# Causal mask, batch order and second-chunk gates at the start of an mLSTM and GELU kernel

## The chip, the cores and the metric

The kernel runs on one core of a Trainium2 chip. A core has five engines that each take their own instructions in order: TensorE (PE; the loading of its weights is shown apart as PEld), VectorE (DVE), ScalarE (ACT), GpSimd (POOL) and SyncE (SP). All DMAs of this kernel are issued by SP. The engines wait for each other by semaphores. The metric is the device time of one execution in microseconds (us), as the median of several runs. The profile is that of one execution.

## The reference

Two stages follow each other. The first is an mLSTM cell over 4 batches, 8 heads, 768 steps and a head width of 40:

```python
for t in range(S):
    m_new = np.maximum(f_gate[:, :, t] + m, i_gate[:, :, t])
    f_stab = np.exp(f_gate[:, :, t] + m - m_new)
    i_stab = np.exp(i_gate[:, :, t] - m_new)
    m = m_new
    C = f_stab[:, :, None, None] * C + i_stab[:, :, None, None] * np.einsum('bhd,bhe->bhde', vt, kt)
    n = f_stab[:, :, None] * n + i_stab[:, :, None] * kt
    h_tilde = np.einsum('bhde,bhe->bhd', C, qt)
    nq = np.einsum('bhd,bhd->bh', n, qt)[:, :, None]
    denom = np.maximum(np.abs(nq), 1.0)
    o = 1.0 / (1.0 + np.exp(-o_gate[:, :, t]))
    y[:, :, t] = o * h_tilde / denom
```

Its result is laid out as 3072 tokens of 320 values and goes through a feed-forward block of width 2048:

```python
h = x @ w_in
g = h * (1.0 / (1.0 + np.exp(-1.702 * h)))
return (g @ w_out).astype(np.float32)
```

q, k, v and the gates come in 32-bit floats, the two weight matrices in 64-bit floats.

## The kernel before

**Chunks.** The 768 steps are cut into 6 chunks of 128 (`w`), and each chunk is done for all 4 batches. Inside a chunk the recurrence is replaced by matrices: decay weights between each pair of steps, times the scores of k and q, times v, plus what the state of the earlier chunks gives. Between chunks `new_states` and `carry` bring the state on.

**The attention steps of a batch.** `transposes(w, b)` makes kT and qT (in chunk 0 by TensorE into p_t and a copy by ScalarE, line 316). `weights(0, b)` builds the exponents of the decay weights in PSUM by matmuls with `pick`, m3 and a3 (lines 333 and 334), and ScalarE takes their exp (line 335); then GpSimd's `affine_select` (line 342) sets to zero what lies in the future. `scores` multiplies k by q into p_s (line 353), and VectorE multiplies the result into the weights (line 355). `values` multiplies by v into p_o (line 365), and VectorE makes y of it with the denominator and the output gate (lines 388 to 394); GpSimd copies 64 columns of y to fill its last third (line 396). `seam` transposes y into p_x (line 403), and ScalarE copies it to xT (line 404). `columns` makes the per-step factors, and `scale_values` multiplies v by some of them on GpSimd (line 410), for the states.

**The gates.** `gates(w)` (lines 245 to 287) runs scans on VectorE. For chunk 0 it also splits two rows into three bf16 parts each: a3 with GpSimd, m3 with VectorE. For later chunks it sends the row m_run to DRAM (m_row), and `spread` loads it back to all partitions.

**The weights.** The 64-bit numbers are turned into 32-bit ones on the chip. `fetch(n)` loads piece n (512 KB), and `convert(n)` makes it on ScalarE (two instructions, "A", lines 233 and 234) and then on VectorE (four, "V", lines 237 to 242). Pieces 0 to 9 belong to w_in, 10 to 19 to w_out. Hidden blocks j = 0 and 1 need the pieces 0, 1 and 2, blocks 2 and 3 the pieces 2, 3 and 4.

**The feed-forward steps.** `up(w, j, n)` multiplies xT by w_in for n pairs of hidden blocks: `full` for the first 256 of the 320 rows (line 467), `rest` for the last 64 (line 473), then the GELU on ScalarE (line 477). `down` multiplies by w_out. The attention of the next chunk is woven into `down`.

**What sets the order.** The order is written by hand: every engine, and SP's queue of DMAs, takes its instructions in the order in which the program names them, and a pool's buffers come round in that order too. p_t, p_w, p_s, p_o, p_x, p_cols and p_c share one pool of four PSUM buffers, ps_a. Chunk 0 is written out, from `gates(0)` to `gate_out(3)`: the steps of the four batches interleaved with `convert(0)`, `convert(1)` and `convert(2)` and with `keep_busy`, matmuls of zeros that keep TensorE running. Then `up(0, 0, 2, between)` does hidden blocks 0 and 1 in two halves: for the first two batches (columns 0 to 255) as soon as their xT is there, with `values(0, 2)`, `values(0, 3)`, both `seam`s and two conversions called in between (the three functions of `between`), and then for the last two. `gates(1)` comes after it, and then SP's loads of k for the next chunk.

At the start SP loads, in this order: gates of chunk 0; k and q of batch 0 and of batch 1; piece 0; v and o of batch 0; k and q of batch 2; v and o of batch 1; piece 1; k and q of batch 3; piece 2; v and o of batches 2 and 3; pieces 3, 4 and 5; gates of chunk 1; pieces 6 to 9.

GpSimd clears, in this order: padding of k_st and q_bl, a column of v_st set to one, then after the gates of chunk 0 state and k_bl, and q_bl once more after the first `up`. VectorE makes `pick` (line 201) and then `half`, `dec_in`, `par` and `pair` (lines 207 to 213), which the gates and columns of later chunks need, ahead of `gates(0)`.

Of the kernel before, what the change touches and what calls it, by code (L numbers as in the profile page):

```python
# [8 lines left out]
FP = mybir.dt.float32  # L9
U32 = mybir.dt.uint32  # L10
BF = mybir.dt.bfloat16
# [11 lines left out]
L = 128  # L23
# [11 lines left out]
def kernel(  # L35
# [131 lines left out]


    load_gates(0)
    for what, n in (("kq", 0), ("kq", 1), (fetch, 0), ("vo", 0), ("kq", 2), ("vo", 1), (fetch, 1), ("kq", 3), (fetch, 2),  # L170
                    ("vo", 2), ("vo", 3), (fetch, 3), (fetch, 4), (fetch, 5)):
        if what is fetch:
            fetch(n)
        else:
            load(0, what, slice(n, n + 1))
    load_gates(1)
    for n in range(6, 10):
        fetch(n)

# [18 lines left out]
    for j in range(3):  # L200
        V.tensor_scalar(out=pick[j * BH:(j + 1) * BH, :], in0=ident[0:BH, 0:BH], scalar1=-1.0, scalar2=None,
                        op0=OP.mult)


    half = const.tile([3 * BH, 2, 64], FP, name="half")
    dec_in = const.tile([3 * BH, 2, BH // 2], FP, name="dec_in")
    V.memset(half, 0.0)
    V.memset(dec_in, 0.0)
    par = const.tile([BH, 2], FP, name="par")
    pair = const.tile([BH, BH // 2], FP, name="pair")  # L210
    V.tensor_reduce(out=par, in_=ident[0:BH, 0:BH].rearrange("p (j two) -> p two j", two=2), axis=AX.X, op=OP.add)
    V.tensor_reduce(out=pair, in_=ident[0:BH, 0:BH].rearrange("p (j two) -> p j two", two=2), axis=AX.X, op=OP.add)
    V.tensor_copy(out=half[0:BH], in_=par.unsqueeze(2).to_broadcast([BH, 2, 64]))
    for t in (k_st, q_st):
        G.memset(t[:, :, D:DP], 0.0)

    a3 = const.tile([3 * BH, L], BF, name="a3")
    m3 = const.tile([3 * BH, L], BF, name="m3")
# [106 lines left out]
    def weights(w, b):  # L325
        if w == 0:
            x = wt[w, b] = work.tile([L, NP, 2, L], FP, tag="wt", bufs=4, name="wt")
            for i in range(2):
                pw = ps_a.tile([L, NP, L], FP, tag="a", name="p_w")
                for p in range(NP):  # L330
                    h = b * H + 2 * p + i
                    one = pick[:, h:h + 1].to_broadcast([3 * BH, L])
                    T.matmul(pw[:, p, :], one, m3, start=True, stop=False)
                    T.matmul(pw[:, p, :], a3, one, start=False, stop=True)
                A.activation(out=x[:, :, i, :], in_=pw, func=AF.Exp)
        else:
            x = wt[w, b].rearrange("s p i t -> s (p i) t")
            for h in range(H):
                A.activation(out=x[:, h, :], in_=x[:, h, :], func=AF.Exp, scale=-1.0,  # L339
                             bias=cols[w][:, b * H + h:b * H + h + 1])  # L340
        x = wt[w, b].rearrange("s p i t -> s (p i) t")
        G.affine_select(out=x, in_=x, compare_op=OP.is_ge, fill=0.0, base=0, pattern=[[0, H], [1, L]],  # L342
                        channel_multiplier=-1)
        if w and b == 0:
            A.activation(out=eo[w], in_=eo[w], func=AF.Tanh, scale=0.5)

    def scores(w, b):
# [9 lines left out]
    def values(w, *bs, states=False):  # L357
        po, pi = {}, {}
        for b in bs:
            po[b] = ps_a.tile([L, H, D1], FP, tag="a", name="p_o")  # L360
            for p in range(NP):
                for i in range(2):
                    h = 2 * p + i
                    for t in HALVES:
                        T.matmul(po[b][t, h, :], wt[w, b][:, p, i, t], v_st[:, b * H + h, :], start=True, stop=True)  # L365
        for b in bs if w else ():
            pi[b] = ps_a.tile([L, H, D1], FP, tag="a", name="p_i")
            for p in range(NP):
                for t in HALVES:
                    T.matmul(pi[b][t, 2 * p:2 * p + 2, :].rearrange("p a b -> p (a b)"), qT[w, b][:, p, t],  # L370
                             state[:, b * NP + p].rearrange("p a b -> p (a b)"), start=True, stop=True)
        if states:

            for b in bs:
                scale_values(w, b)
            new_states(w)
            for b in bs:
                scale_state(w, b)
        for b in bs:
            u = po[b]  # L380
            if w:
                u = work.tile([L, H, D1], FP, tag="u", name="u")
                g = cols[w][:, BH + b * H:BH + (b + 1) * H].unsqueeze(2).to_broadcast([L, H, D1])
                V.tensor_tensor(out=u, in0=pi[b], in1=g, op=OP.mult)
                V.tensor_tensor(out=u, in0=po[b], in1=u, op=OP.add)

            den = work.tile([L, H, 1], FP, tag="den", name="den")
            V.tensor_scalar(out=den, in0=u[:, :, D:D1], scalar1=-1.0, scalar2=1.0, op0=OP.mult, op1=OP.max)
            V.tensor_tensor(out=den, in0=u[:, :, D:D1], in1=den, op=OP.max)
            V.reciprocal(out=den, in_=den)  # L390
            z = eo[w][:, b * H:(b + 1) * H, :]
            V.scalar_tensor_tensor(out=z, in0=z, scalar=1.0, in1=u[:, :, 0:D], op0=OP.add, op1=OP.mult)
            y = ys[w, b] = work.tile([L, DM + 64], FP, tag="y", name="y")
            V.scalar_tensor_tensor(out=y[:, 0:DM].rearrange("p (h d) -> p h d", d=D), in0=z, scalar=0.5,
                                   in1=den.to_broadcast([L, H, D]), op0=OP.mult, op1=OP.mult)
            G.tensor_copy(out=y[:, DM:DM + 64], in_=y[:, DM - 64:DM])
# [55 lines left out]
    def up(w, j, n, between=None, states=False):  # L452

        x = xT[w].rearrange("p c b t -> p c (b t)")
        begin, end = range(j, j + n // 2), range(j + n // 2, j + n)
        ph = {}
        ts = slice(0, W)

        def take(j, pool, tag):
            ph[j] = [pool.tile([128, W], FP, tag=tag, name="p_h") for _ in range(2)]

        def full(j, first):
            for c in range(2):
                for i in range(2):
                    T.matmul(ph[j][i][:, ts], w_half[i][c][:, j // 2, j % 2 * 128:(j % 2 + 1) * 128], x[:, c, ts],  # L467
                             start=(first and c == 0), stop=(not first and c == 1))

        def rest(j, first):  # L470
            for i in range(2):
                r = slice(i * 64, i * 64 + 64)
                T.matmul(ph[j][i][:, ts], w_in_x[r, j, :], x[r, 2, ts], start=first, stop=not first)

        def gelu(j):
            for i, g in enumerate(hidden_of(w, j)):
                A.activation(out=g, in_=ph[j][i], func=AF.Gelu_apprx_sigmoid)  # L477

        if between:
            take(j, ps_m, "m")  # L480
            take(j + 1, ps_x, "x")
            ts = slice(0, W // 2)
            full(j, True)
            between[0]()
            rest(j, False)
            rest(j + 1, True)
            between[1]()
            full(j + 1, False)
            between[2]()
            ts = slice(W // 2, W)  # L490
        for k in begin:
            if k not in ph:
                take(k, *((ps_m, "m") if k == j else (ps_x, "x")))
            full(k, True)
        if states:
            new_states(w)
            carry(w)
# [197 lines left out]
        z = eo[0][:, b * H:(b + 1) * H, :]  # L695
        A.activation(out=z, in_=z, func=AF.Tanh, scale=0.5)

    G.memset(v_st[:, :, D:D1], 1.0)
    gates(0)
    G.memset(state, 0.0)  # L700
    G.memset(k_bl, 0.0)
    transposes(0, 0)
    weights(0, 0)
    transposes(0, 1)
    convert(0, "A")
    scores(0, 0)
    weights(0, 1)
    keep_busy(2)
    convert(0, "V")
    scores(0, 1)  # L710
    keep_busy(2)
    gate_out(0)
    transposes(0, 2)
    values(0, 0)
    weights(0, 2)
    keep_busy(2)
    gate_out(1)
    convert(1, "A")
    values(0, 1)
    scores(0, 2)  # L720
    seam(0, 0)
    transposes(0, 3)
    weights(0, 3)
    convert(1, "V")
    seam(0, 1)
    convert(2)
    scores(0, 3)
    columns(0)
    gate_out(2)
    gate_out(3)  # L730


    beside = {0: ((5,), range(10, 16)), 1: ((6, 7, 8), ()), 2: ((9, 10, 11), (16, 17)), 3: ((12, 13, 14), (18, 19)),
# [14 lines left out]
    for w in range(NW):  # L748
        more = w + 1 < NW
        for j in range(NF // 2):  # L750
            if j % 2 == 0:
# [4 lines left out]
                        else:  # L756
                            up(w, j, 4, states=(j == 0))
                elif j == 0:
                    up(w, j, 2, (lambda: values(0, 2), lambda: values(0, 3),
                                 lambda: (seam(0, 2), seam(0, 3), convert(3), convert(4))))  # L760
                    for b in range(B):
                        scale(0, b)
                    weights_in(0)
                else:
                    weights_in(j // 2)
                    up(w, j, 2, states=(j == 2))
            if j == 0 and more:
                load(w + 1, "o")
            if w == 0 and j == 0:
                gates(1)  # L770
                load_blocks(1, 0)
                spread(1)
            if w == 1 and j == 1:
# [2 lines left out]
            if more:  # L776
# [7 lines left out]
                        spread(w + 1)  # L784
                if j == (4 if w else 6):
                    load(w + 1, "k")
                if w == 0 and j == 0:
                    G.memset(q_bl, 0.0)
                if w == 1 and 4 <= j < 6:
                    transposes(w + 1, 2 * j - 8)  # L790
                    transposes(w + 1, 2 * j - 7)
# [68 lines left out]
```

## Time and profile before

| | us |
|---|---|
| median of 5 runs | 494.01 |
| lowest and highest run | 493.92 and 496.68 |
| the profiled execution's own time | 494.01 |
| its span in the profile | 492.3 |
| TensorE busy | 482.8 |
| VectorE busy | 332.5 |
| ScalarE busy | 207.1 |
| GpSimd busy | 69.2 |

The span runs from the first to the last recorded instruction. Busy time is a mean over stages that differ, so it has to be read by stage. In a timeline a row gives the start, the duration, the engine, the source line, the operation with what it writes and reads, and how many instructions the row merges; in brackets stands how long the engine had idled before and what ended the idling. A matmul of 32-bit numbers is two records, so "x16" can be eight instructions. A row of waits gives the time in total, the number of waits and the longest.

### The profile page before, as it was taken

The numbers are of one execution on the slowest core, as the hardware profiler recorded it, in microseconds if no ns is written. First come the engines' busy times: TensorE is split into PE (matmuls) and PEld (weight loads), VectorE is DVE, ScalarE is ACT, GpSimd is POOL, SyncE is SP. The second block draws the span as 40 slices with busy tenths as digits, with TensorE's granted clock in tenths as the row PEclk, the third lists the DMA queues.
The fourth block names the chain that finished last, engine by engine and source line by source line (L and its number), as shares of the span: only waits on it lengthen the run. The fifth ranks groups of instructions, "written<-read, shape, count | busy, mean of one in ns | idle before, by whom it ended". The sixth has DMA issues, their size and how long they took to land. (4 is left out here: it accounts for less than half of the span.)

```text
span 492.3 us, 10268 instructions
## 1 busy us (share of the span) xinstructions
PE 482.8 (98%) x4030; PEld 387.5 (79%) x4030; DVE 332.5 (68%) x817; ACT 207.1 (42%) x533; POOL 69.2 (14%) x109
## 2 busy tenths in 40 slices
PE   8899999999999999999999999999999999999997
PEld 5674457775446999877999877999977999877897
DVE  6879985882792777686696586786666776244841
ACT  4557668311224700465901374910354930155400
POOL 7240001231000332000232000242000030000000
PEclk9999999999999999999999999999999999999999
DMA  9999799403699610796300497300194000000000
GB/s 148 177 253 352 87 278 164 60 15 67 73 166 206 78 34 3 120 246 74 31 28 3 88 259 84 40 23 8 49 270 43 2 1 28 28 0 3 0 28 27
DMA packets 175952, 44.85 MB, mean 91 GB/s; under 512 B 164352, under 2 KB 169504, under 8 KB 175904
## 3 DMA queue, kind: packets, MB, share of 16 engines
q1 hardware_dynamic: 175904, 44.21, 48.2%
q8 instruction: 31, 0.51, 0.4%
q14 instruction: 17, 0.14, 0.1%
HBM read 40.17 MB, written 4.01 MB: 90 GB/s over the span
## 5 line engine op out<-in xcount | busy, mean ns | idle before, releaser
L643 PE MATMUL p_out<-w_out_sb,g 128*128 128x160 f32 x480 | 69.8, 301 | 0.0
L404 ACT COPY xT<-p_x 128x384 f32<-128x384 f32 x24 | 11.0, 481 | 134.3 <-PE p_x L403 134.3
L643 PEld LDWEIGHTS p_out<-w_out_sb,g 128*128 128x128 f32 x480 | 66.3, 190 | 1.3 <-issue 0.5
L467 PE MATMUL p_h<-xT,w_in_sb 128*128 128x512 f32 (+1 forms) x144 | 58.1, 553 | 2.1 <-ACT xT L404 1.2
L342 POOL TENSOR_SCALAR_AFFINE_SELECT wt<-wt 128x1024 f32<-128x1024 f32 x24 | 27.2, 1132 | 230.2 <-ACT wt L339 226.8
L552 DVE TENSOR_TENSOR g<-p_u,g 128x256 f32<-128x256 f32 x64 | 27.2, 424 | 40.8 <-PE p_u L544 32.8
L467 PEld LDWEIGHTS p_h<-xT,w_in_sb 128*128 128x128 f32 x144 | 26.4, 190 | 31.5 <-issue 26.8
L648 DVE TENSOR_TENSOR o_sb<-o_sb,p_out 128x160 f32<-128x160 f32 x70 | 21.4, 317 | 41.2 <-PE p_out L643 40.9
L549 ACT COPY g<-p_u 128x256 f32<-128x256 f32 x96 | 34.4, 377 | 34.5 <-PE p_u L544 31.2
L339 ACT ACTIVATE wt<-wt,cols 128x128 f32<-128x128 f32 x160 | 48.0, 397 | 0.0
L556 ACT ACTIVATE g<-g 128x256 f32<-128x256 f32 x96 | 33.9, 425 | 31.3 <-DVE g L552 31.3
L355 DVE TENSOR_TENSOR wt<-p_s,wt 128x512 f32<-128x512 f32 x48 | 30.5, 683 | 11.0 <-POOL wt L342 9.1
L592 PE MATMUL p_out<-w_out_sb,g 128*128 128x320 f32 x128 | 36.2, 437 | 0.0
L643 PE MATMUL p_out<-t,big 128*128 128x160 f32 x240 | 35.5, 301 | 0.0
L477 ACT ACTIVATE g<-p_h 128x512 f32<-128x512 f32 x32 | 17.9, 598 | 38.7 <-PE p_h L467 20.0
L643 PEld LDWEIGHTS p_out<-t,big 128*128 128x128 f32 x240 | 33.3, 190 | 0.2
L592 PEld LDWEIGHTS p_out<-w_out_sb,g 128*128 128x128 f32 x128 | 23.8, 190 | 10.1 <-issue 0.5
L544 PE MATMUL p_u<-xT,w_in_sb 128*128 128x256 f32 x128 | 31.2, 382 | 0.0
L544 PE MATMUL p_u<-xs,big 128*128 128x256 f32 x128 | 30.3, 379 | 0.0
L572 PE MATMUL p_v<-xT,w_in_x 64*128 64x512 f32 x64 | 29.6, 602 | 0.0
L572 PE MATMUL p_u<-xT,w_in_x 64*128 64x512 f32 x64 | 29.6, 602 | 0.0
L365 PEld LDWEIGHTS p_o<-v_st,wt 128*64 128x64 f32 x768 | 24.1, 138 | 5.1 <-issue 2.7
(156 smaller groups left out, 852.8 us busy)
## 6 DMA issues: line engine op xcount, KB each, us to landing
wt<-m_row SPq DMA_DIRECT2D x20, 512.0 KB, 6.2
out_dram<-o_sb SPq DMA_DIRECT2D x24, 160.0 KB, 1.8
eo<-in_o_gate_dram SPq DMA_DIRECT2D x5, 640.0 KB, 5.6
v_st<-in_v_dram SPq DMA_DIRECT2D x5, 640.0 KB, 8.8
k_st<-in_k_dram SPq DMA_DIRECT2D x5, 640.0 KB, 11.1
big<-in_moe_w_in_dram SPq DMA_DIRECT2D x5, 512.0 KB, 5.9
big<-in_moe_w_out_dram SPq DMA_DIRECT2D x8, 320.0 KB, 4.5
k_bl<-in_k_dram SPq DMA_DIRECT2D x40, 64.0 KB, 2.7
```

The source lines that it names most:

```text
L339: A.activation(out=x[:, h, :], in_=x[:, h, :], func=AF.Exp, scale=-1.0, bias=cols[w][:, b * H + h:b * H + h + 1])
L342: G.affine_select(out=x, in_=x, compare_op=OP.is_ge, fill=0.0, base=0, pattern=[[0, H], [1, L]], channel_multiplier=-1)
L355: V.tensor_tensor(out=wt[w, b][:, :, i, :], in0=pw[i], in1=wt[w, b][:, :, i, :], op=OP.mult)
L365: T.matmul(po[b][t, h, :], wt[w, b][:, p, i, t], v_st[:, b * H + h, :], start=True, stop=True)
L467: T.matmul(ph[j][i][:, ts], w_half[i][c][:, j // 2, j % 2 * 128:(j % 2 + 1) * 128], x[:, c, ts], start=(first and c == 0), stop=(not first ...
L544: T.matmul(p[k][:, ts[t]], a[:, k // 2, k % 2 * 128:(k % 2 + 1) * 128], b, start=first, stop=True, skip_group_check=True)
L549: A.copy(out=g[k][i][:, ts[t]], in_=chain[k][:, ts[0]])
L552: V.tensor_tensor(out=g[k][i][:, ts[t]], in0=p[k][:, ts[pt]], in1=g[k][i][:, ts[t]], op=OP.add)
L556: A.activation(out=dst, in_=dst if src is None else src, func=AF.Gelu_apprx_sigmoid)
L572: T.matmul(p[k], w_in_x[r, k, :], x[r, 2, :], start=False, stop=True, skip_group_check=True)
L592: T.matmul(po, gs[w, f // 2][:, f % 2, b * L:(b + 1) * L], w_out_sb[:, f, :], start=(f == 0), stop=(f == NF - 1))
L643: T.matmul(po, a(f), b[:, f, :], start=(f == 0), stop=(f == NH - 1))
```

## The change

1. **Mask.** In chunk 0 the causal mask is added to the exponents by TensorE: each group of four heads in PSUM starts with one matmul of a bf16 identity (`ident_bf`) with a bf16 matrix `not_yet`, which holds −1e30 where the step lies in the future and zero elsewhere. The matmuls for the heads add to it. The select on GpSimd after the exp is gone for chunk 0 and stays for the others. VectorE clears `not_yet` and makes `ident_bf`; GpSimd's `affine_select` fills `not_yet`. Both lie in `xs`, which is free then.
2. **Order of chunk 0.** Batches 0 and 1 go all the way to xT first (weights, scores, values, seam), and then batches 2 and 3. `convert(0)` on VectorE comes behind the y of both, `convert(1)` behind it; `convert(2)` moves behind the last seam. Both scores of batches 2 and 3 come before any of hidden blocks 0 and 1.
3. **The first `up`.** `between` is now one function. `full` for columns 0 to 255 of blocks 0 and 1 comes first, then `rest_of_first` (`values` of batches 2 and 3 together, both seams, conversions 2, 3 and 4), then `full` for columns 256 to 511, then `rest` for all columns. `scale` is called per batch earlier, and `values(0, 2, 3, states=True)` scales v of batches 2 and 3.
4. **Second chunk's gates.** `load_gates(1)` moves ahead of v and o of batch 0, and `gates(1)` into chunk 0's order, between `transposes(0, 1)` and `scores(0, 0)`; with it its DMA of m_row moves ahead of the loads of pieces 10 to 15.
5. **Loads.** Order now: gates of chunk 0; k and q of batches 0 and 1; gates of chunk 1; v and o of batches 0 and 1; piece 0; k and q of batch 2; piece 1; k and q of batch 3; v and o of batches 2 and 3; pieces 2 to 9.
6. **Clearings.** k_bl's clearing and v_st's column of ones move ahead of `gates(0)`, state's behind the values of batch 0; the second clearing of q_bl is gone. `half`, `dec_in`, `par` and `pair` are made behind `gates(0)`.

```diff
@@ loads
+    for what, n in (("kq", 0), ("kq", 1), (load_gates, 1), ("vo", 0), ("vo", 1), (fetch, 0), ("kq", 2), (fetch, 1),
+                    ("kq", 3), ("vo", 2), ("vo", 3), *((fetch, n) for n in range(2, 10))):
@@ before gates(0)
     for t in (k_st, q_st):
         G.memset(t[:, :, D:DP], 0.0)
+    G.memset(v_st[:, :, D:D1], 1.0)
+    G.memset(k_bl, 0.0)
+
+    not_yet, ident_bf = (xs.bitcast(BF)[:, i * L:(i + 1) * L] for i in range(2))
+    V.memset(not_yet, 0.0)
+    G.affine_select(out=not_yet, in_=not_yet, compare_op=OP.is_ge, fill=NEG, base=0, pattern=[[1, L]],
+                    channel_multiplier=-1)
+    V.tensor_copy(out=ident_bf, in_=ident)
@@ weights(0, b)
+                T.matmul(pw, ident_bf, not_yet.unsqueeze(1).to_broadcast([L, NP, L]), start=True, stop=False)
                 for p in range(NP):
                     h = b * H + 2 * p + i
                     one = pick[:, h:h + 1].to_broadcast([3 * BH, L])
-                    T.matmul(pw[:, p, :], one, m3, start=True, stop=False)
-                    T.matmul(pw[:, p, :], a3, one, start=False, stop=True)
+                    T.matmul(pw[:, p, :], one, m3, start=False, stop=False)
+                    T.matmul(pw[:, p, :], a3, one, start=False, stop=(p == NP - 1))
                 A.activation(out=x[:, :, i, :], in_=pw, func=AF.Exp)
+            return
@@ the order of chunk 0, after
+    gates(0)
+    (half, dec_in, par, pair)
+    transposes(0, 0)
+    weights(0, 0)
+    transposes(0, 1)
+    gates(1)
+    scores(0, 0)
+    weights(0, 1)
+    scores(0, 1)
+    gate_out(0)
+    gate_out(1)
+    values(0, 0)
+    G.memset(state, 0.0)
+    convert(0, "A")
+    values(0, 1)
+    keep_busy(2)
+    seam(0, 0)
+    transposes(0, 2)
+    convert(0, "V")
+    seam(0, 1)
+    convert(1, "A")
+    weights(0, 2)
+    keep_busy(2)
+    transposes(0, 3)
+    weights(0, 3)
+    convert(1, "V")
+    columns(0)
+    gate_out(2)
+    gate_out(3)
+    scale(0, 0)
+    scale(0, 1)
+    scores(0, 2)
+    scores(0, 3)
+
+    def rest_of_first():
+        values(0, 2, 3, states=True)
+        seam(0, 2)
+        seam(0, 3)
+        for n in (2, 3, 4):
+            convert(n)
@@ up, with between
+            begin, end = (j, j + 1), ()
         for k in begin:
+            take(k, *((ps_m, "m") if k == j else (ps_x, "x")))
+            full(k, True, slice(0, W // 2 if between else W))
+        if between:
+            between()
+            for k in begin:
+                full(k, True, slice(W // 2, W))
@@ after the first up
-                gates(1)
                 load_blocks(1, 0)
                 spread(1)
...
-                if w == 0 and j == 0:
-                    G.memset(q_bl, 0.0)
```

## The prediction

> **What bounds the kernel now.** I read the page's head first, then the busy time by stage, then TensorE's waits from 44 us to the end, then the timelines of the first 45 us. Two lines of the page and the windows:
>
> ```profile
> span 492.3 us, 10268 instructions
> ...
> PE 482.8 (98%) x4030; PEld 387.5 (79%) x4030; DVE 332.5 (68%) x817; ACT 207.1 (42%) x533; POOL 69.2 (14%) x109
> ```
>
> ```profile
> core 0: us, PE busy (x) PEld busy (x) DVE busy (x) ACT busy (x) POOL busy (x), PEclk, DMA share, GB/s
> 0.00:10.00 10.00, 8.15 (x44) 4.64 (x44) 7.65 (x26) 3.76 (x6) 6.98 (x19) 1.00 0.91 146
> 10.00:20.00 10.00, 8.14 (x130) 6.50 (x130) 6.46 (x13) 5.59 (x12) 3.58 (x5) 1.00 1.21 180
> 20.00:25.80 5.80, 5.62 (x83) 4.91 (x80) 4.73 (x11) 4.61 (x10) 1.88 (x3) 1.00 1.00 160
> 25.80:40.00 14.20, 12.83 (x120) 9.92 (x120) 11.35 (x21) 8.17 (x18) 5.99 (x8) 1.00 0.99 278
> 40.00:44.20 4.20, 3.89 (x12) 1.35 (x13) 3.79 (x8) 4.20 (x9) 0.00 (x0) 1.00 1.06 397
> 44.20:116.00 71.80, 71.80 (x522) 45.91 (x523) 57.09 (x116) 33.54 (x75) 10.61 (x16) 1.00 0.63 129
> ```
>
> The waits of TensorE from 44 us to the end:
>
> ```profile
> PE p_h L467 <- ACT xT L404: 0.6, 1, 0.6
> PE p_out L643 <- DVE o_sb L648: 0.4, 1, 0.4
> ```
>
> From 44.2 us on TensorE has no gap up to 116 and 1.0 us of waits in all. So nothing that the change does to work beside TensorE after 44 us (gates of the second chunk, SP's queue, the clearing of q_bl) can gain more than that 1.0 us. The change is worth what it does to one moment: when `new_states(0)` (p_c, line 429) may start, 44.13 us now. Everything behind it follows at TensorE's pace.
>
> TensorE on the way there:
>
> ```profile
> 24.58 1.18 PE L353 MATMUL p_s<-qT,kT 40*128 40x128 f32 x16
> ...
> 32.94 0.82 PE L403 MATMUL p_x<-ident,y 128*128 128x128 f32 x6
> 34.38 1.99 PE L467 MATMUL p_h<-xT,w_in_sb 128*128 128x256 f32 x8 [0.62 <-ACT xT L404]
> ...
> 39.95 1.95 PE L467 MATMUL p_h<-xT,w_in_sb 128*128 128x512 f32 x4 [0.59 <-DVE w_in_sb L242]
> 42.21 1.98 PE L467 MATMUL p_h<-xT,w_in_sb 128*128 128x512 f32 x4 [0.31 <-DVE w_in_sb L242]
> ```
>
> The last scores end at 25.76; 18.4 us later p_c starts. The loads bound the first part, as the view of q's tile shows: q of batch 3 was issued at 14.40 and took the longest of the four, 7.9 us, so it landed at 22.3.
>
> ```profile
> DMA to landing us min/median/max: 3.9/4.6/7.9
> ```
>
> The start, on GpSimd and VectorE:
>
> ```profile
> 1.31 0.74 POOL L215 MEMSET k_st<- 128x768 f32 x1
> 1.99 0.74 POOL L215 MEMSET q_bl<- 128x768 f32 x1
> 2.67 0.16 POOL L698 MEMSET v_st<- 128x32 f32 x1
> ...
> L201 DVE TENSOR_SCALAR pick<-ident x3: 173/173/1449, 1.4 to 3.1; 32x32 bf16<-32x32 f32 x3
> ```
>
> The first of three equal `pick` copies took 1449 ns, from 1.40 to 2.85, the others 173: it ended when GpSimd's three clearings did (2.67 + 0.16 = 2.83).
>
> **What the Trainium skill says.** "SBUF — State Buffer", section Who interferes with whom: VectorE in a two-port mode and GpSimd share one port pair, held for a whole instruction while the other blocks. The 1449 ns agree, and so does the shift of line 238 at 35.66, 2.58 us against 0.43 elsewhere, while q_bl is cleared (36.17 to 37.97). "TensorE: Matmul & The Clock Gate", section What's actually happening: the clock falls after about 3.4 us of idling. No gap here is that long and every slice shows full clock; my longest gap below is 2 us.
>
> **The change, part by part.**
>
> *Mask on TensorE.* Removed: four GpSimd selects of 1.09 to 1.50 us between exp and the scores' product (line 342, first chunk). Only batch 0's lay on the path: the product waited for it from p_s's end at 11.08 to 12.20, 1.1 us. Added: eight matmuls 128x512 bf16. The trace has that shape as p_idle, two in 0.60 us; estimate 0.22 to 0.30 each, 2.1 us in all, of which per batch one stands before data that is late anyway and one, 0.22, on the path. Without that cover a batch costs 0.6.
>
> *k_bl's clearing moved ahead of gates(0), half's making behind it.* The clearing takes 1.80 us (q_bl's row, same shape) and now follows v_st's at 2.83 back to back, to about 4.6. `pick` is two-port, and all three copies must be through before not_yet's clearing, the bf16 identity and the gate scans. Pick's first copy was passed over at two such boundaries in this trace; even if it slips in at the third, the next two block. So picks end at 4.6 + 0.39 = 5.0 (3.22 before); not_yet and identity 0.4; gates(0) starts at 5.4 instead of 3.75: 1.65 late. Bounds: 0 (VectorE slips in ahead of k_bl each time) to 2.0 (the new select blocks it too). I take 1.65. The making of half (0.44 us, 3.31 to 3.75) moves behind gates(0).
>
> *Through the first two batches.* a3 is ready 4.3 after the gates start (3.75 to 8.04 before): 9.7. Weights(0,0): 9.7 to 10.9, exp to 11.5. Scores 11.6 to 12.8. VectorE meanwhile does gates(0) to 10.1, half to 10.5, gates(1) 2.4 (44.43 to 46.8 before) to 12.9: its move costs the product nothing, with 0.1 to spare; its two loads (issued at 4.3, about 4.5 to land) are there at 8.9. On SP these two, 32 KB, pass ahead of v and o, whose batch 0 then lands near 10 and is wanted at 15.7; fetch(0) lands near 14 and is wanted by ScalarE at 15.4. Products 13.0 to 14.2; scores(0,1) 13.7 to 14.9 (0.75 behind the products' start, as at 12.95); products to 16.3; p_o; the y chains of 1.47 each to 17.7 and 19.1 (21.6 + 0.5 = 22.1 before, since convert(0) stood ahead). TensorE's p_x at 17.95 and 19.45; ScalarE copies xT, kT, qT, xT to 20.55, convert(1) to 21.65, exp(0,2) to 22.7.
>
> *Batches 2 and 3.* The same loads stand ahead of q's last one, in another order, so it lands at 22.3 again. Transposes to 22.95, qT to 23.7, exp(0,3) to 24.75, columns to 25.05 (p_s's fourth buffer). The last scores end at 26.6: 0.8 late. So half of the 1.65 is won back by the mask and the order, and 22.3 + 3.4 = 25.7 is the best that this load allows.
>
> *The middle.* Now four half blocks (full(0), full(1), 3.85 us by twice the 1.92 of eight records) go ahead of p_o(2) and p_o(3): 26.6 to 30.45; p_o to 32.6 (1.13 each). Then nothing is left on TensorE to cover the y chains: y of batch 2 to 33.05, of batch 3 to 34.5 (1.47 each), the pad copy and p_x to 35.3, ScalarE's xT to 35.9; second halves from 36.0. Before, full(1), rest(0) and rest(1) lay in those holes, and the second halves started at 34.38. Then 3.85 + rest at full width 1.99 = 5.85 (before 4.98, from 34.38 to 39.36, and 0.59 of waiting): full(2) at 41.85, its second half at 43.8, p_c at **45.75**. VectorE's three conversions after xT(3): start 36.5, 2.36 each, 43.6; just in time. They no longer meet GpSimd's scale and clearing, which cost line 238 2.15 us.
>
> Sum at p_c: +0.8 (last scores 26.6 against 25.76), +0.8 (from them to the second halves 9.4 against 8.6: y chains uncovered), 0 (from there to p_c 9.75 both times: 0.87 more of rest against waits of 0.59 and 0.31 gone) = 45.75 − 44.13 = **+1.6 us**.
>
> *Second chunk.* SP waited 4.1 us for the gates at m_row and then issues k_bl; that goes, and q_bl comes some 4 us earlier. VectorE's wait for it (2.8 us, up to 79.74) shrink, but TensorE has no gap: 0. VectorE loses 2.4 us of gates between conversions 4 and 6; with PE 1.6 later, its lead grows from 1.8 us (w_in piece 6 at 49.2, wanted at 51.0). So no new stall. q_bl's clearing (1.80) and GpSimd's freed time: 0.
>
> Span 492.3 + 1.6 = 493.9; the run took 494.01 around that span, and this is also the median, so **495.6**.
>
> **The rivals.**
>
> A. The hold is carried in full. If the two-port casts of gates(0) or the handovers in the longer chain win nothing back, scores end at 27.4 or later, and +1.65 +0.8 or more gives 2.5 to 3.5: **497.0**, slower by over 0.5%. For it: about fourteen handovers follow one another. Against: mask and convert(0) leave the path. It decides from scores ending at 27.5.
>
> B. q of batch 3 lands later. p_t is ready for it at 22.2, so each microsecond is paid in full; at 23.2 or later it makes +2.5: **496.7**. For it: it took 7.9 us, and the queue is full (share 0.9 to 1.2). Against: the same bytes ahead.
>
> C. No hold, and k and q flow faster with fetch(2) behind them: scores end at 25.0 to 25.8, and only the middle's +0.8 is left, or a little less: −1 to +0.4, **494.2**. For it: fetch(2) did share the queue with q before.
>
> D. Faster: the new order fills TensorE. Real work before full(2) is some 30 us (transposes 4.8, weights 3.6, scores 4.6, p_o 4.5, p_x 2.0, columns 0.3, p_h 10.0), and it has 39.95; with q at 20.5 and the y chains hidden, full(2) at 37.0: −2.5 to −3, **491.2**. It decides where the gap between p_o(3) and the second halves stays under 1 us. Against: nothing stands on TensorE's queue there.
>
> **How the numbers follow.** 0.5% of 494 is 2.47 us, about what a measurement tells from no change. My case (+0.4 to +2.4) 0.55, A 0.16, B 0.12, C 0.11, D 0.06. So faster 0.06, same 0.66, slower 0.28. The range runs from −0.6 (C within) to +3.5 (A's end): 493.4 to 497.5; D and the tails are left out.
>
> **What would show it.** Pick's copies ending near 5.0 and the first scan near 5.4; last scores of the first chunk near 26.6; a gap of 3.4 us with only p_x in it before the second halves; p_c near 45.8; no gap on TensorE from there to 116. It would be wrong if pick ended at 3.2, if q of batch 3 landed off 22.3 by over 1 us, or if TensorE waited for a conversion after p_c.

## The result and the profile after

| | before | after |
|---|---|---|
| median, us | 494.02 | 498.12 |
| lowest and highest run | 493.26 and 497.92 | 496.41 and 502.18 |
| profiled execution, its span | 494.01, 492.3 | 498.06, 496.4 |
| mean granted clock in the profiled execution | 0.999 | 0.993 |
| last scores of chunk 0 end | 25.76 | 27.99 |
| second halves of blocks 0 and 1 start | 34.38 | 37.53 |
| p_c starts | 44.13 | 48.16 |

The changed kernel takes 1.0086 times as long, interval 1.007 to 1.0102: slower by 4.1 us. The forecast was 495.6, with a range from 493.4 to 497.5.

The head of the page of the changed kernel:

```profile
span 496.4 us, 10268 instructions
...
PE 486.1 (98%) x4028; PEld 389.8 (79%) x4028; DVE 330.9 (67%) x819; ACT 207.5 (42%) x533; POOL 63.1 (13%) x105
...
PEclk8998999999999999999999999999999999999999
```

TensorE executes two records fewer and is busy 3.3 us longer (482.8 before). The clock row (PEclk, the granted clock in tenths for 40 equal slices of the span) points to the reason: an 8 in the first slice and another in the fourth, where all was 9 before. TensorE's waits from 48.2 us to the end are the two of before, 0.6 and 0.4, so the whole loss lies ahead of p_c, which is 4.03 late.

TensorE of the changed kernel on the way to p_c, in the timeline:

```profile
25.79 2.20 PE L347 MATMUL p_s<-qT,kT 40*128 40x128 f32 x32
27.92 3.72 PE L462 MATMUL p_h<-xT,w_in_sb 128*128 128x256 f32 x16
31.57 2.07 PE L359 MATMUL p_o<-v_st,wt 128*64 128x41 f32 x64
34.96 0.54 PE L398 MATMUL p_x<-ident,y 128*128 128x128 f32 x3 [1.32 <-DVE den L383]
36.42 0.53 PE L398 MATMUL p_x<-ident,y 128*128 128x128 f32 x3 [0.93 <-DVE y L389]
37.53 5.16 PE L462 MATMUL p_h<-xT,w_in_sb 128*128 128x256 f32 x16 [0.57 <-ACT xT L399]
...
48.16 1.43 PE L424 MATMUL p_c<-v_st,k_st 128*40 128x41 f32 x64
```

The two `p_h` rows have the same shape and the same count, and one takes 3.72 us and the other 5.16. The gap ahead of the slow one is the one forecast: p_o ends at 33.64, and until 37.53 TensorE has only two short p_x.

TensorE of the changed kernel by stretches (start:end, length, busy time, records, granted clock, share of the DMA engines, GB/s):

```profile
6.10:9.50 3.40, 1.55 (x10) 1.00 1.37 153
9.50:13.00 3.50, 3.50 (x24) 0.54 1.12 207
...
33.60:37.00 3.40, 1.11 (x8) 1.00 1.02 242
37.00:40.40 3.40, 2.87 (x7) 0.51 1.05 393
40.40:44.00 3.60, 3.60 (x17) 0.99 0.74 240
```

Twice TensorE does little for some 3.4 us while its clock is whole, and in the next 3.4 us it works, at half clock. The first fall lies under batch 0's weights and scores, the second under the second halves.

The executions of the changed kernel fall on levels by their mean granted clock. No run of it had a whole clock:

| mean granted clock | runs | time, us | (1 − clock) × 495 |
|---|---|---|---|
| 0.997 | 6 | 496.41 to 496.70 | 1.5 |
| 0.993 | 11 | 497.66 to 498.31 | 3.5 |
| 0.989 | 2 | 499.62 to 499.67 | 5.4 |
| 0.983 | 5 | 502.15 to 502.18 | 8.4 |

The time climbs by 5.7 us from the first level to the last, while 6.9 us more of clock are lost. Followed back to a clock of 1.0, the line ends near 495.3. What the kernel takes without the falls is measured below.

### The profile page after: what moved, and what is told of

It reads as the page before. It is cut to its first block, busy times and chain, and to the rows that moved or that the text cites. A ratio compares the mean times of both kernels' runs of the same rounds, so it can differ in the third digit from the quotient of the medians.

```text
span 496.4 us, 10268 instructions
## 1 busy us (share of the span) xinstructions
PE 486.1 (98%) x4028; PEld 389.8 (79%) x4028; DVE 330.9 (67%) x819; ACT 207.5 (42%) x533; POOL 63.1 (13%) x105
## 5 line engine op out<-in xcount | busy, mean ns | idle before, releaser
L462 PEld LDWEIGHTS p_h<-xT,w_in_sb 128*128 128x128 f32 x144 | 27.7, 197 | 30.8 <-issue 26.8
L336 POOL TENSOR_SCALAR_AFFINE_SELECT wt<-wt 128x1024 f32<-128x1024 f32 x20 | 22.4, 1120 | 226.8 <-ACT wt L334 224.6
L534 PEld LDWEIGHTS p_u<-xT,w_in_sb 128*128 128x128 f32 x128 | 23.7, 190 | 4.5 <-DVE o_sb L638 1.5
```

Source lines behind the costliest of these rows:

```text
L534: T.matmul(p[k][:, ts[t]], a[:, k // 2, k % 2 * 128:(k % 2 + 1) * 128], b, start=first, stop=True, skip_group_check=True)
```

## The experiments

The question is what the 4.1 us are made of. Theory C is the clock (it is not the forecast's rival C): the sum of the forecast stands, and the stretches where TensorE is partly busy halve its clock. Its rivals are the forecast's other terms: that the held `pick` costs more than reckoned (rival A of the forecast, H in the texts ahead of the runs), that the uncovered y chains do, or that handovers and loads came later (L). Times are medians. The first five kernels below are the changed kernel with an edit, then two versions built on it, then five are the kernel before with an edit.

**x1_clearing_late.** k_bl's clearing behind the gates: it no longer holds `pick`, and so there is no stretch of little work at 6 us.

```diff
     G.memset(v_st[:, :, D:D1], 1.0)
-    G.memset(k_bl, 0.0)
...
     gates(0)
+    G.memset(k_bl, 0.0)
```

> The changed kernel with k_bl's clearing put behind gates(0) again. Theory C (the excess over the forecast is TensorE at half clock, set off by gaps): the first scan starts at 3.5 instead of 5.1, the gap before the first weights shrinks below 1 us, the clock no longer falls at 10 to 13 us, the last scores end near 26.0 instead of 28.0; the fall at 37 to 41 stays possible. Time 496.0 to 496.8, against 498.1 for the changed kernel. Rival H (the hold alone, carried in full, no clock in it): the same gain of 1.6 from the hold only, 496.5, and the granted clock unchanged. Rival L (later handovers and loads): no more than 0.5 gained, 497.6 or above.

Measured: 497.28 (1.0071 of before, 1.0052 to 1.009). The front is cured: from 6.0 to 9.4 TensorE is busy for 3.21 of 3.40 us, the clock stays whole there, and the last scores end at 25.91, 2.1 us earlier. p_c gains only 0.8 (47.33 against 48.16), because the middle now falls for two windows. TensorE of this kernel in the timeline, and then by stretches:

```profile
35.78 6.08 PE L461 MATMUL p_h<-xT,w_in_sb 128*128 128x256 f32 x16 [0.57 <-ACT xT L398]
...
47.33 1.43 PE L423 MATMUL p_c<-v_st,k_st 128*40 128x41 f32 x64
```

```profile
34.00:37.40 3.40, 2.49 (x7) 0.50 1.06 209
37.40:40.80 3.40, 3.40 (x10) 0.53 1.03 334
```

TensorE works all through the second stretch and still runs at half clock. The time lies above what theory C gave for this kernel: the middle lost two windows of clock and not one.

The clearing also has a price where it now stands. VectorE's last instruction of `gates(0)`, 0.28 us in the changed kernel, runs here while k_bl is cleared (7.73 to 9.54):

```profile
7.76 1.85 DVE L275 TENSOR_SCALAR st<-st,m_run 32x128 f32<-32x128 f32 x1
```

So x1 takes the hold off `pick`, but puts one of about the same length ahead of `gates(1)`.

**x2_fill_middle, x3_fill_front, x4_fill_both.** The changed kernel with matmuls of zeros in the middle gap, in the front one, and in both. Nothing is moved and no wait is taken away.

```diff
     transposes(0, 0)
+    keep_busy(8)                       # x3, x4
     weights(0, 0)
...
         values(0, 2, 3, states=True)
+        fill(5)                        # x2, x4: matmuls 128x512 bf16 into a tile p_fill of ps_a
         seam(0, 2)
+        fill(3)
         seam(0, 3)
+        fill(2)
```

> The changed kernel with ten matmuls of zeros put on TensorE around the two seams of batches 2 and 3 (five, three and two), where it waits for y and xT; they go into a buffer of their own. Theory C: the second fall of the clock (37 to 41 us) goes, the second half blocks take 3.7 instead of 5.2 us, 1.0 to 1.5 us gained where it had fallen: 496.6 to 497.1, and the mean granted clock rises. Rivals H and L: nothing gained, 498.1, since the matmuls only fill idle time; or up to 0.4 lost where they delay p_x.

> The changed kernel with eight matmuls of zeros put ahead of weights(0, 0), where TensorE waits for the gates; the hold of VectorE stays. Theory C: the first fall of the clock (10 to 13 us) goes, the transposes of batch 1 take 0.6 instead of 1.06 us, the last scores end near 26.6 instead of 28.0: 496.5 to 496.9. Rivals H and L: nothing gained, 498.1.

> The changed kernel with both fillings. Theory C: no fall of the clock, mean granted clock 0.999 and the runs close together, 495.4 to 495.8, the forecast's own sum. Rivals H and L: 498.1, with the same spread over several levels.

Measured: x2 496.98 (1.0065, 1.0041 to 1.009), x3 496.73 (1.0058, 1.0035 to 1.008), x4 **495.44** (1.0034, 1.0023 to 1.0045). All twelve runs of x4 lie between 495.39 and 495.61, with clocks of 0.999 and 1.0: the levels are gone. TensorE of x4 in the timeline, and by stretches:

```profile
24.19 2.22 PE L347 MATMUL p_s<-qT,kT 40*128 40x128 f32 x32
...
35.95 3.72 PE L462 MATMUL p_h<-xT,w_in_sb 128*128 128x256 f32 x16
...
45.62 1.43 PE L424 MATMUL p_c<-v_st,k_st 128*40 128x41 f32 x64
```

```profile
6.00:9.40 3.40, 2.84 (x15) 1.00 1.34 149
...
33.00:36.40 3.40, 2.85 (x15) 1.00 1.04 257
```

The second halves take 3.72 again. The hold is still there (the first `pick` took 3157 ns, as in the changed kernel), and the y chains are as uncovered as before; only zeros were put beside them. So theory C is shown: of the 4.03 us at p_c, 48.16 − 45.62 = 2.54 are the clock in these two executions. The last scores end at 26.41 instead of 27.99, which puts 1.58 in the front, and the remaining 0.96 in the middle. The other 45.62 − 44.13 = 1.49 are the change itself.

x3 shows the middle alone: its front is whole, and the second halves take 5.41. In x2 the middle is whole, and the front is left as it was. In its profiled execution TensorE is busy for only 1.27 us from 6.0 to 9.4, and yet the clock did not fall there; in 6 of x2's 13 runs the mean clock is 0.997 or lower, in the other 7 it is not. The same stretch falls in some executions and not in others. x2's profiled run (496.91) has p_c at 45.58, as x4, but is longer: 4.4 us lie behind TensorE's last work where the changed kernel has 3.0. The last store of the result took 3.2 us there from issue to landing, and 1.8 in x4, so this part of x2's time has nothing to do with the clock.

**x5_late_and_fill.** x1's edit and x2's together: `pick` not held, and a filled middle.

> The changed kernel with k_bl's clearing behind gates(0) and the ten matmuls of zeros around the two seams. Theory C: with the clock kept up in the middle, what the hold itself costs shows alone: last scores of the first chunk at 25.9 as in the run with the late clearing (26.4 with both fillings and the hold), so 0.5 us less than with both fillings: 494.9, mean clock 0.999. If the hold were worth its whole 1.4 us at the end: 494.0.

Measured: 495.18 (1.0023, 1.0009 to 1.0036); 14 of 22 runs have a clock of 0.999 or 1.0, and 11 of them lie between 494.98 and 495.11. Against x4's 495.44 a free `pick` is then worth about 0.45 us. This is not the whole price of the clearing, which here too holds the last instruction of `gates(0)` for 1.85 us; no run leaves it out. (x4 and x5 ran on two chips, on which the kernel before took 493.95 and 494.00.) In its profiled execution (496.55) the clock fell from 15.4 to 18.8, after a stretch, 12.0 to 15.4, with 2.47 of 3.40 us busy.

**z1_half_between.** x1, and in the middle no zeros but real work: hidden block 1's first half goes behind p_o of batches 2 and 3, beside the y chains.

```diff
             full(k, True, slice(0, W // 2 if between else W))
+            if between:
+                between[k - j]()       # values_of_rest behind block 0, seams_of_rest behind block 1
         if between:
-            between()
             for k in begin:
...
-    def rest_of_first():
+    def values_of_rest():
+        convert(2, "A")
         values(0, 2, 3, states=True)
+        convert(2, "V")
+
+    def seams_of_rest():
         seam(0, 2)
         seam(0, 3)
-        for n in (2, 3, 4):
-            convert(n)
+        convert(3)
+        convert(4)
```

> The changed kernel with k_bl's clearing late and the first half of full(1) moved behind p_o of batches 2 and 3, so that real work lies beside their y chains, and convert(2) ahead of them on ScalarE and behind them on VectorE. No zeros are added. Theory C: the gap of 3.4 us before the second halves shrinks to about 1.5, the clock stays up, the second halves start near 33.4 to 34 and p_c near 43 to 43.6: 492.8 to 493.6. If the uncovered y chains were not what the middle costs: 494.9 or more.

Measured: **492.97** (0.999, 0.9978 to 1.0002), not told apart from before. TensorE of this kernel in the timeline:

```profile
23.72 2.19 PE L346 MATMUL p_s<-qT,kT 40*128 40x128 f32 x32
...
29.77 1.99 PE L461 MATMUL p_h<-xT,w_in_sb 128*128 128x256 f32 x8
...
33.85 3.72 PE L461 MATMUL p_h<-xT,w_in_sb 128*128 128x256 f32 x16 [0.57 <-ACT xT L398]
...
43.05 1.43 PE L423 MATMUL p_c<-v_st,k_st 128*40 128x41 f32 x64
```

x5, with zeros in the same place, took 495.0 where its clock did not fall, so the real work is worth 2.0 us more. From the end of the last scores to the second halves it is 33.85 − 25.91 = 7.9 us, against 9.5 in x4: 1.6 of the 1.9 us of the work that was moved. From the same end to p_c it is 17.1 against 19.2, so another 0.5 is gained behind the start of the second halves. There x4 waits 0.20 us for a conversion and z1 for none; z1 also has conversion 2 earlier, and the two moves were not tried apart.

**z2_gates_later.** z1, and `gates(1)` taken out from ahead of batch 0's product.

```diff
     transposes(0, 1)
-    gates(1)
     scores(0, 0)
...
     convert(1, "V")
+    gates(1)
     columns(0)
```

> The kernel of the run with full(1)'s half between, and the second chunk's gates(1) moved from ahead of the first scores' product to behind the VectorE part of convert(1). There the product of batch 0 waited for VectorE from 10.9 to 12.46. If gates(1) stood on the path: product at 11.0, last scores 0.5 to 1.0 earlier than 25.9, 492.0 to 492.5, bounded by q of batch 3. If that load bounds the front anyway: 492.9.

Measured: **492.47** (0.9971, 0.9958 to 0.9983), faster than both kernels. All 22 runs have a clock of 1.0. TensorE of this kernel in the timeline:

```profile
21.22 0.63 PE L306 MATMUL p_t<-ident,q_bl 128*128 128x128 f32 x4 [0.51 <-DMA q_bl<-in_q_dram]
...
42.38 1.43 PE L423 MATMUL p_c<-v_st,k_st 128*40 128x41 f32 x64
```

So `gates(1)` ahead of the product cost 0.5 us in z1. VectorE comes to it late there, as the moved clearing holds the instruction ahead of it for 1.85 us: the product of batch 0 starts at 12.46 in z1 and at 11.03 here. The clock agrees: from 12.0 to 15.4 TensorE is busy for 2.47 of 3.40 us in z1, which lost some clock in 9 of 22 runs, and for 3.21 here. q of batch 3 is awaited until 21.22 here, which is a microsecond before the 22.3 that the forecast took as the best this load allows.

**b1_clearing_early.** The kernel before with one line moved: k_bl's clearing ahead of `gates(0)`.

```diff
     G.memset(v_st[:, :, D:D1], 1.0)
+    G.memset(k_bl, 0.0)
     gates(0)
     G.memset(state, 0.0)
-    G.memset(k_bl, 0.0)
```

> The kernel before with one part of the change alone: k_bl's clearing ahead of gates(0). Theory C: the first scan starts at 5.4 instead of 3.75, the first weights 1.6 later, TensorE idles about 3 us there and the clock may fall at 10 to 13 us; the later loads absorb part: 494.6 to 496.4, with more than one level. If the hold is absorbed by the load of q: 494.0.

Measured: 498.37 (1.008, 1.0053 to 1.0108). That one line costs as much as the whole change. The first `pick` took 3156 ns, and TensorE of this kernel by stretches shows what came of it:

```profile
5.20:8.60 3.40, 1.68 (x10) 1.00 1.33 193
8.60:12.00 3.40, 2.47 (x19) 0.52 1.08 198
12.00:15.40 3.40, 3.40 (x25) 0.50 1.37 163
15.40:18.80 3.40, 3.40 (x26) 0.50 1.05 209
18.80:22.20 3.40, 3.40 (x21) 0.50 1.07 194
```

The clock is halved from about 8.7 to 22.3, four windows, though TensorE is busy throughout the last three. The last scores end at 31.32, 5.6 us late, and p_c comes at 48.29, 4.2 late: 1.4 is won back because VectorE's shift beside q_bl's clearing took 0.84 us in this execution and not 2.58 (see b4). The lowest of its nine runs, at a clock of 0.997, is 495.36, 1.4 above before; which way that shift went there is not known, so what the late gates alone cost here stays open. The fall itself is shown on the other kernel, without the change's new order.

**b2_mask_tensor.** The kernel before with the mask on TensorE and nothing else of the change.

```diff
+                T.matmul(pw, ident_bf, not_yet.unsqueeze(1).to_broadcast([L, NP, L]), start=True, stop=False)
...
                 A.activation(out=x[:, :, i, :], in_=pw, func=AF.Exp)
+            return
```

> The kernel before with the mask alone: the mask matmuls on TensorE in chunk 0 and no select on GpSimd there. The product of batch 0 starts 1.1 us earlier, but the chain is bound by the load of q of batch 3 at 22.3 from there on: 493.5 to 494.2. If the mask's eight matmuls stood on the path: 495.5 or more; if the select was what bound the front: 492.9.

Measured: 493.53 (0.9982, 0.997 to 0.9995), p_c 0.47 earlier (43.66). The mask gains half a microsecond. The product of batch 0 starts at 11.43 instead of 12.20, and later TensorE waits 0.47 us for q of batch 3, until 22.26; so the select's 1.1 us doesn't come through whole.

**b3_gates_early.** The kernel before with the second chunk's gates loaded and computed early.

```diff
-    for what, n in (("kq", 0), ("kq", 1), (fetch, 0), ...
+    for what, n in (("kq", 0), ("kq", 1), (load_gates, 1), (fetch, 0), ...
...
     transposes(0, 1)
+    gates(1)
     convert(0, "A")
```

> The kernel before with the second chunk's gates alone moved: their two loads behind k and q of batch 1, gates(1) between transposes(0, 1) and convert(0). The product of batch 0 waits for GpSimd's select until 12.2 there, and gates(1) on VectorE is through by about 12: 494.0, with SP's 4.1 us wait at m_row gone. If the early m_row and k loads were worth something: 493.0 or less. If gates(1) delays the product: 494.5 to 495.

Measured: 494.24 (1.0005, 0.9982 to 1.0028): no difference is seen. Its runs lie on two levels, four at 492.8 and eight at 494.0 to 494.6, besides two that lost clock; b4 takes this up.

**b4_no_clearing.** The kernel before without q_bl's second clearing.

```diff
-                if w == 0 and j == 0:
-                    G.memset(q_bl, 0.0)
```

> The kernel before without the second clearing of q_bl, one of the change's edits alone. In its trace VectorE's shift of line 238 stood 2.58 us, until that clearing was over, and TensorE then waited 0.59 and 0.31 us for conversions; in a run where the shift slipped in ahead of the clearing these waits were gone and p_c started at 42.9. If that is so: 492.6 in nearly every run, 1.4 less, without a second level at 494.0. The prediction's price for this edit (no gain of its own): 494.0.

Measured: median 492.79 against 493.98, but the ratio's interval holds 1 (0.9996, 0.9982 to 1.0011), so the times alone show no gain. The expectation of 492.6 in nearly every run missed: 11 of 22 runs lie at 492.57 to 492.65, and three that kept their clock at 493.90 to 494.09. What the clearing can cost is seen in single executions. VectorE's timeline without the clearing, and TensorE's:

```profile
35.64 0.85 DVE L238 TENSOR_SCALAR w_in_sb<-w_in_sb 128x512 uint32<-128x512 uint32 x1
```

```profile
42.70 1.43 PE L429 MATMUL p_c<-v_st,k_st 128*40 128x41 f32 x64
```

The shift of line 238 takes 0.85 instead of 2.58, TensorE no longer waits 0.59 and 0.31 for conversions, and p_c comes 1.43 earlier. The kernel before itself ran at 492.6 in 8 of the 42 executions measured beside b4, and most often at 494.0. In b3's profiled execution (492.8) the shift had taken its turn ahead of the clearing: 0.84, and the clearing 2.08 instead of 1.80, with p_c at 42.91. So by these traces the clearing costs about 1.4 us where GpSimd comes first and nothing where VectorE does. That this turn makes the two levels of the kernel before is likely but not shown, and b4's three runs near 494 are not explained.

**b5_no_filling.** The kernel before without its three `keep_busy(2)` in chunk 0.

```diff
     weights(0, 1)
-    keep_busy(2)
     convert(0, "V")
     scores(0, 1)
-    keep_busy(2)
     gate_out(0)
...
     weights(0, 2)
-    keep_busy(2)
     gate_out(1)
```

> The kernel before without its six matmuls of zeros in the middle of chunk 0 (three calls of keep_busy(2)); those ahead of the first weights stay. Theory C: TensorE's gaps at 12, 14 and 18.5 to 19.4 us grow by 0.5 each, the clock may fall there in part of the runs: 494.0 with levels of 495.5 and more. Rivals H and L: 494.0 or less, since six matmuls leave the queue.

Measured: 492.52 (0.9978, 0.9966 to 0.9989), faster by 1.5. Theory C had let the clock fall here, and it was wrong for this kernel: 21 of 22 runs have a clock of 0.999 or 1.0. From 12.0 to 15.4 TensorE is busy for 2.33 of 3.40 us and keeps its clock in nearly every run, whereas x5 and z1, with 2.47 in the same stretch, lost some clock in 8 and 9 of their 22 runs (where, only x5's profiled run shows). TensorE's last scores of chunk 0:

```profile
23.07 1.18 PE L353 MATMUL p_s<-qT,kT 40*128 40x128 f32 x16
```

They end at 24.25, 1.5 us earlier, and q of batch 3 is used at 21.26 without a wait for its load. The waits of 0.57 and 0.31 us for conversions are still there (p_c at 42.60), so this is not the lower level of the kernel before. The zeros had stood on the path.

The moment of p_c accounts for nearly all of these times. Differences to before, in us, with the median or, where the runs spread, the profiled run beside p_c of that same run:

| kernel | p_c | p_c − 44.13 | time − 494.0 |
|---|---|---|---|
| after | 48.16 | +4.0 | +4.1 |
| x1 | 47.33 | +3.2 | +3.2 (profiled run) |
| x3 | 46.67 | +2.5 | +2.7 |
| x4 | 45.62 | +1.5 | +1.4 |
| b1 | 48.29 | +4.2 | +4.2 (profiled run) |
| b2 | 43.66 | −0.5 | −0.5 |
| z1 | 43.05 | −1.1 | −1.0 |
| b4 | 42.70 | −1.4 | −1.4 (profiled run) |
| b5 | 42.60 | −1.5 | −1.5 |
| z2 | 42.38 | −1.8 | −1.7 (profiled run) |

The profiled runs of b3 (42.91, −1.2 at p_c and in the time) and of x5 (46.03, +1.9 and +2.5) go with these. x2's does not: +1.5 at p_c and +2.9 in the time, with its late last store.

## Why the prediction was wrong

**The step that failed** is the sentence "No gap here is that long and every slice shows full clock; my longest gap below is 2 us." The Trainium skill, "TensorE: Matmul & The Clock Gate", section What's actually happening, puts the fall after at least one idle window of about 3.4 us, and says too that the clock follows how busy TensorE has been of late and that the window is free-running. The forecast read "idle" as no work at all and compared single gaps with 3.4. In the changed kernel TensorE's longest single wait is 1.4 us, and the clock fell after stretches of 3.4 us with 1.55 and 1.11 us of work in them. The forecast itself had written that until the second halves there is "a gap of 3.4 us with only p_x in it". It had that stretch and did not price it, and it did not add up the work around its wait for the late gates either. The measured price is 2.54 us at p_c and 495.44 → 498.12 in the time.

**What held.** With the clock kept up (x4) the steps met their marks: last scores ending at 26.41 (forecast 26.6), second halves at 35.95 (36.0), p_c at 45.62 (45.75), time 495.44 (495.6). The gates' start was late by the mechanism named, by 1.35 us and not by 1.65. In the changed kernel GpSimd and VectorE show, in the timeline and in the view of pick's tile:

```profile
2.73 1.80 POOL L203 MEMSET k_bl<- 128x2048 f32 x1
...
5.10 0.40 DVE L244 TENSOR_TENSOR_SCAN f_run<-one,fi 32x128 f32<-32x128 f32 x1
```

```profile
L198 DVE TENSOR_SCALAR pick<-ident x3: 172/173/3157, 1.4 to 4.8; 32x32 bf16<-32x32 f32 x3
```

The first copy was passed over until the clearing ended at 4.53, and the other two then ran through, so that the scan started at 5.10 and not at 5.4. a3's last operation ended at 9.38 (forecast 9.7), 4.28 after the gates' start as forecast. The 3157 ns agree with what the Trainium skill, "SBUF — State Buffer", section Who interferes with whom, says of the port pair that VectorE and GpSimd share. Also right: from p_c on nothing is gained or lost by the gates, the queues or the clearing of the second chunk.

The three terms of the sum held too, each within 0.15 us. Between before and x4 the last scores end 0.65 later (forecast +0.8), from there to the second halves it takes 0.92 more (+0.8), and from there to p_c 0.08 less (0). For `gates(1)` the forecast gave no cost, with 0.1 to spare. VectorE of x4 in the timeline:

```profile
12.46 0.22 DVE L281 TENSOR_SCALAR dec_in<-pair,both 32x16 f32<-32x16 f32 x1
12.75 1.29 DVE L349 TENSOR_TENSOR wt<-p_s,wt 128x512 f32<-128x512 f32 x2
```

`gates(1)` is through at 12.68, and the product starts 0.11 behind p_s's end at 12.64; in z2, where VectorE stands idle there, it also starts 0.11 behind that end. So it cost nothing beside the held `pick`.

**Right sums over other parts.** Some parts of these terms were not as forecast.
- The hold was put at 1.65 at the gates with half of it won back later. It was 1.35, and with `pick` freed (x5) the time is 0.45 less.
- q of batch 3 landed at about 21.9 in the changed kernel, and the 22.3 of the forecast was no bound that this load sets: z2 has it at 21.22, and b5, with the loads in the order of before, uses it at 21.26 without a wait. What brings it earlier there was not followed.
- The forecast took off the waits of 0.59 and 0.31 for q_bl's clearing. Without it alone (b4) p_c came 1.4 earlier, so half a microsecond more lay there.
- SP was to come to q_bl about 4 us earlier. In the trace after, it stands 6.7 us in three waits for weight pieces to be converted, k_bl's loads begin at 50.27 against 50.77, and VectorE waits for q_bl's 2.20 us up to 83.18. No cost and no gain came of it.

**The rivals.** The point from which A decides, scores ending at 27.5, was passed (27.99), but by the clock: x4 has the hold in full and ends them at 26.41. B, C and D did not occur. D wanted the y chains hidden, and z1 builds that in part, with work under them: it makes the change even with before rather than slower.

**What stays open.** Which stretches fall. After 1.1 to 1.7 us of work in 3.4 the clock fell in the profiled executions of the changed kernel, x1, x3 and b1, but not in x2's (1.27). With 2.3 to 2.5 it fell in x5's, and kept whole in z1's and b5's. After 2.8 or more no fall was found, and the kernel before has a stretch with 1.97 (15.0 to 18.4) that kept its clock. A free-running window would make the outcome hang on where its edges lie, which fits the levels of the same kernel, but no run here shows the edges, and no threshold was measured.

## What to carry to other kernels

Where an order leaves TensorE only partly busy, add up its busy time over stretches of about 3.4 us, not the single gaps: here some 1.1 to 1.7 us of work in one could halve the clock of the next, and the two falls of the changed kernel cost 1.6 and 1.0 us. Zeros kept the clock and gave back only that, and where the clock would not have fallen they cost (b5); real work moved beside the wait gave 2 us more (z1, with a conversion moved too). Before a clearing on GpSimd is moved, look at which VectorE instruction will meet it, and at what stands behind that instruction: `pick` in the changed kernel, the end of `gates(0)` in x1.

## What the runs showed that was not expected

- A clock fall can outlast a stretch of full work: in b1 three stretches in which TensorE was busy for 3.40 of 3.40 us passed at a clock of 0.50, in x1 one. With such a run of windows b1's last scores came 5.6 us late, though one line of the kernel was moved.
- Between GpSimd instructions that follow one another VectorE does not reliably get its turn. `pick` was passed over at three boundaries in the changed kernel (3157 ns instead of 173), and in x3 its three copies took 172, 1350 and 1823; the shift beside q_bl's clearing took 2.58 us in the trace of the kernel before and 0.84 in those of b1 and b3. By these traces one such turn is worth about 1.4 us.
- Six matmuls of zeros, two in 0.60 us, cost the kernel before 1.5 us, though TensorE seemed to have time there.
